# Gathering the 32-column matmuls of a LayerNorm backward stage into one place per pair of rows

## The chip, the cores and the metric

One core of one Trainium2 chip. The metric is the time of one execution in microseconds (us), as the device counts it; the lower the better. "Stage" below is the LayerNorm 2 backward stage, measured in a trace from the start of the last matmul of the gate and up projections in the main loop to the first matmul of the next transform. It is about 6% of the kernel.

## The reference, cut to what matters

The kernel computes a block with two LayerNorms, a spectral (FFT) filter and a gated bilinear feed-forward part, and all gradients of it. Only this much matters here:

```python
def _layernorm(x, axis=-1, eps=1e-05): ...
h = _layernorm(x) * (1 + ca) + sa
x = x + ga * _A_ref(h, A_w_r, A_w_i)       # rfft2 * W, irfft2
h = _layernorm(x) * (1 + cb) + sb          # LayerNorm 2
x = x + gb * _B_ref(h, ...)                # (h Wg) * (h Wu), times Wd
# reference = jax.vjp of this: the output and gradients by A_x, A_w_r, A_w_i,
# B_w_gate, B_w_up, B_w_down, c, w_mod; x is 2048 x 576
```

The backward stage of LayerNorm 2 takes the gradient by h, of 16 rows of tiles (128 x 576 each), and makes of it (1) column sums for the gradient of the modulation, (2) the gradient by x, multiplied and folded, whose (3) transform along the 16 rows of tiles starts the backward FFT.

Of the kernel before, what the change touches and what calls it, by code (L numbers as in the profile page):

```python
# [81 lines left out]
def build(ctx, tc, A_x, A_w_r, A_w_i, B_w_gate, B_w_up, B_w_down, c_in, w_mod, grad_out,  # L82
          out_0, out_1, out_2, out_3, out_4, out_5, out_6, out_7, out_8):
    nc = tc.nc
    pe, ve, ac, po, sp = nc.tensor, nc.vector, nc.scalar, nc.gpsimd, nc.sync
# [124 lines left out]
    with tc.manual_schedule(engines={PE}):  # L210
# [115 lines left out]
        def single():  # L326
            sbank[0] = (sbank[0] + 1) % 3
            return sbank[0]
# [112 lines left out]
        def stage_a(fj, b):  # L441
            for m in range(4):
                mm(bank[:, b, 128 * m:128 * m + 128], fj[:, FB[m]:FB[m] + 128], bdf, True, True)

        def stage_a_rem(fj, b, sub):
            mm(bank[0:32, b, 128 * sub:128 * sub + 128], fj[:, 256:288], bdf, True, True)
            mm(bank[32:64, b, 128 * sub:128 * sub + 128], fj[:, 544:576], bdf, True, True)

        def evac_a(eng, b, j):
            dst = At[:, 0:4, :, 8 * j:8 * j + 8]  # L450
            src = bank[:, b, :].rearrange("p (m c b) -> p m c b", m=4, c=16)
            if eng is ac:
                ac.copy(dst, src)
            else:
                ve.tensor_copy(dst, src)

        def evac_rem(eng, brem, j0, n):
            dst = At[0:64, 4, :, 8 * j0:8 * (j0 + n)].rearrange("p c (j b) -> p j c b", j=n)
            src = bank[0:64, brem, 0:128 * n].rearrange("p (j c b) -> p j c b", j=n, c=16)
            if eng is ac:  # L460
                ac.copy(dst, src)
            else:
                ve.tensor_copy(dst, src)
# [47 lines left out]
        def load_W(t, u):  # L511
            for ri, src in enumerate((A_w_r, A_w_i)):
                if u == 0:
                    rows = bass.AP(src.tensor, src.offset, [[16 * DF, 128], [8 * DF, 2], [1, DF]])
                    sp.dma_start(t[:, :, ri, 0:DF], rows)
                else:
                    sp.dma_start(t[:, 0, ri, 0:DF], src[u::16, :])
                    po.indirect_dma_start(out=t[:, 1, ri, 0:DF], out_offset=None, in_=src[:, :], in_offset=rev_rows, element_offset=(16 - u) * DF)
# [100 lines left out]
        for jg in range(4):  # L619
# [8 lines left out]
            for jj in range(4):  # L628
                b = single()
# [156 lines left out]
        def sbk():  # L786
            sbank[0] += 1
            return sring[sbank[0] % len(sring)]
# [148 lines left out]
        def acc_b(j):  # L937

            return acc[:, j, 0:288].bitcast(BF)
# [20 lines left out]
        def gh2_last(j):  # L960

            for h in range(2):
                b = sbk()
                gh2_mms(NP - 1, j, h, bank[:, b, 0:288])
                hs = slice(288 * h, 288 * h + 288)
                tt(acc_b(j)[:, hs], acc[:, j, hs], bank[:, b, 0:288], ADD)
# [57 lines left out]
        def quarter_sums(a, b, q, start, stop):  # L1024

            for h in range(2):
                r = slice(32 * (q + h), 32 * (q + h) + 32)
                mm(bank[r, b, 0:288], ones[:, 0:32], a[:, 288 * h:288 * h + 288], start, stop, skip_group_check=True)
# [14 lines left out]
        def load_n(j):  # L1043
            if j < 14:
                sp.dma_start(acc_h(j), n_d[:, j, :])

        def load_yl(i):
            yl[i] = yl_r.next()
            sp.dma_start(yl[i][:], y_d[:, 2 * i:2 * i + 2, :])
# [7 lines left out]
        def load_wdr(i0, i1):  # L1057
            sp.dma_start(wdr[:, i0:i1, :], B_w_down[128 * i0:128 * i1, :].rearrange("(j f) d -> f j d", f=128))
# [44 lines left out]
        st_a = {}  # L1103
# [4 lines left out]
        def front(i):  # L1108
            gn, t2, q, s = gn_r.next(), t2_r.next(), q_r.next(), s_r.next().rearrange("p (k v) -> p k v", k=2)
            n, opc = n_pair(i), two(mod[:, SCB, :])  # L1110
            tt(gn[:], b_pair(i), opc, MUL)
            tt(q[:], b_pair(i), n, MUL)
            tt(t2[:], q[:], opc, MUL)
            for k in range(2):
                j = 2 * i + k
                act(gn[:, k, :], gn[:, k, :], ACT.Copy, scale=rstd2[:, j:j + 1], accum_out=s[:, k, 0:1])
                act(t2[:, k, :], t2[:, k, :], ACT.Copy, scale=nrs2[:, j:j + 1], accum_out=s[:, k, 1:2])
            st_a[i] = (gn, t2, q, s)

        def back(i):  # L1120
            gn, t2, q, s = st_a[i]
            gx, n = gx_r.next(), n_pair(i)
            ts(s[:, :, 0], s[:, :, 0], -1.0 / D, None, MUL)
            for k in range(2):
                act(t2[:, k, :], n[:, k, :], ACT.Identity, bias=s[:, k, 0:1], scale=s[:, k, 1:2])
            tt(gn[:], gn[:], t2[:], ADD)
            tt(gx[:], gn[:], go[:, 2 * i:2 * i + 2, :], ADD)
            sp.dma_start(gx1_d[:, 2 * i:2 * i + 2, :], gx[:])
            tt(t2[:], gx[:], two(mod[:, SGA, :]), MUL)
            fold(gn, t2, 2)  # L1130
            tt(t2[:], gx[:], yl[i][:], MUL)

        def sums_1(j):
            quarter_sums(acc_b(j), 2, 0, j == 0, j == 15)
            quarter_sums(st_a[j // 2][2][:, j % 2, :], 2, 2, j == 0, j == 15)

        def sums_2(i):
            for k in range(2):
                quarter_sums(st_a[i][1][:, k, :], 5, 2 * k, i == 0, i == 7)

        def row_a(j):
            Fj = st_a[j // 2][0]
            b = sbk()
            stage_a(Fj[:, j % 2, :], b)
            evac_a(ac, b, j)
            if j % 2:
                b = sbk()
                for i in range(2):
                    stage_a_rem(Fj[:, i, :], b, i)
                evac_rem(ac, b, j - 1, 2)  # L1150

        def load_third(t, name, k):
            n = 1536
            sp.dma_start(t.rearrange("p a b c -> p (a b c)")[:, n * k:n * k + n], tabs[name][:, n * k:n * k + n])
# [6 lines left out]
        for j in range(19):  # L1161
            want = min(16, 3 + 5 * j // 4)
            while done < want:
                gh2_last(done)
                done += 1
                if done < want:
                    fill.run(1.0)
            while loaded < min(done, j + 6):
                load_n(loaded)
                loaded += 1  # L1170
            if j % 2 == 0 and j < 16:
                front(j // 2)
                back(j // 2)
                if 2 <= j < 14:
                    load_yl(j // 2 + 1)
            if fill.left() > 12.0 or j > 15:
                fill.run(1.0 if j < 16 else 2.0)
            if 1 <= j < 17:
                sums_1(j - 1)
            if fill.left() > 12.0 or j > 15:  # L1180
                fill.run(1.0)
            if 3 <= j:
                if j % 2 == 0:
                    sums_2(j // 2 - 2)
                row_a(j - 3)
            if j == 4:
                sp.dma_start(TB.rearrange("p a b -> p (a b)"), tabs["TB"][:, :])
            if 6 <= j < 9:
                load_third(TC, "TC", j - 6)
            if j == 12:  # L1190
                for i0 in range(9, 28, 5):
                    load_wdr(i0, min(28, i0 + 5))
                for k in range(3):
                    load_third(TI, "TI", k)
                sp.dma_start(TBI.rearrange("p a b -> p (a b)"), tabs["TBI"][:, :])
            if j == 15:
                for t in W_r.t:
                    po.memset(t[:, :, :, DF:FP], 0.0)
                for u in range(2):
                    Ws[u] = W_r.next()  # L1200
                    load_W(Ws[u], u)
            if j == 16:
                load_wdr(0, 6)
# [172 lines left out]
        for j in range(18):  # L1376
# [31 lines left out]
            while mdone < min(18, 6 * j // 5):  # L1408
                k, i = mdone // 3, mdone % 3
# [4 lines left out]
            if 5 <= j < 14:  # L1414
                i = j - 5
# [101 lines left out]
```

## The kernel before: the parts that the change and the argument touch

TensorE's order is the program's; the order of all other engines is chosen by a scheduler when the kernel is built. `fill` is a queue of matmul work left over from the main loop (weight gradients), drawn on here to keep TensorE busy. Its results need a PSUM bank from the same ring of six that the stage uses (`sbk`), and VectorE or ScalarE has to take them out (by a copy or a multiply) before the bank is free.

```python
def stage_a(fj, b):                       # 128-column matmuls
    for m in range(4):
        mm(bank[:, b, 128 * m:128 * m + 128], fj[:, FB[m]:FB[m] + 128], bdf, True, True)

def stage_a_rem(fj, b, sub):              # 32-column matmuls: the remainder of 576 = 4 x 128 + 2 x 32
    mm(bank[0:32, b, 128 * sub:128 * sub + 128], fj[:, 256:288], bdf, True, True)
    mm(bank[32:64, b, 128 * sub:128 * sub + 128], fj[:, 544:576], bdf, True, True)
# ...
def quarter_sums(a, b, q, start, stop):   # 32-column matmuls: column sums, kept in bank b
    for h in range(2):
        r = slice(32 * (q + h), 32 * (q + h) + 32)
        mm(bank[r, b, 0:288], ones[:, 0:32], a[:, 288 * h:288 * h + 288], start, stop, ...)
# ...
def front(i):                             # VectorE and ScalarE, a pair of rows at a time
    gn, t2, q, s = ...
    n, opc = n_pair(i), two(mod[:, SCB, :])       # n was stored by the main loop, and is loaded here
    tt(gn[:], b_pair(i), opc, MUL)                # L1111
    tt(q[:], b_pair(i), n, MUL)                   # L1112
    tt(t2[:], q[:], opc, MUL)                     # L1113
    for k in range(2):
        j = 2 * i + k
        act(gn[:, k, :], gn[:, k, :], ACT.Copy, scale=rstd2[:, j:j + 1], accum_out=s[:, k, 0:1])
        act(t2[:, k, :], t2[:, k, :], ACT.Copy, scale=nrs2[:, j:j + 1], accum_out=s[:, k, 1:2])
    st_a[i] = (gn, t2, q, s)

def back(i):
    # ... gn += n * s1 + s0 (ScalarE L1125, VectorE L1126); gx = gn + upstream gradient; stored
    tt(t2[:], gx[:], two(mod[:, SGA, :]), MUL)
    fold(gn, t2, 2)                               # L436, L437
    tt(t2[:], gx[:], yl[i][:], MUL)               # L1131

def sums_1(j):
    quarter_sums(acc_b(j), 2, 0, j == 0, j == 15)
    quarter_sums(st_a[j // 2][2][:, j % 2, :], 2, 2, j == 0, j == 15)

def sums_2(i):
    for k in range(2):
        quarter_sums(st_a[i][1][:, k, :], 5, 2 * k, i == 0, i == 7)

def row_a(j):
    Fj = st_a[j // 2][0]
    b = sbk()
    stage_a(Fj[:, j % 2, :], b)
    evac_a(ac, b, j)
    if j % 2:
        b = sbk()
        for i in range(2):
            stage_a_rem(Fj[:, i, :], b, i)
        evac_rem(ac, b, j - 1, 2)
# ...
for j in range(19):
    want = min(16, 3 + 5 * j // 4)
    while done < want:
        gh2_last(done)                            # a row of the gradient by h: 8 matmuls, 2 adds on VectorE
        # ... fill
    # ... loads of n for finished rows
    if j % 2 == 0 and j < 16:
        front(j // 2)
        back(j // 2)
    # ... fill
    if 1 <= j < 17:
        sums_1(j - 1)
    # ... fill
    if 3 <= j:
        if j % 2 == 0:
            sums_2(j // 2 - 2)
        row_a(j - 3)
    # ... loads of tables for the next stage
```

## Time and profile before

| | before |
|---|---|
| time, median of 3 runs | 1496.74 us (1494.34 to 1497.73) |
| span of the profiled run | 1493.0 us |
| stage in its trace | 87.3 us |

The page of the profiled run, cut to the span, TensorE's line and the chain that ended last (followed back from the last instruction; shares of the span):

```profile
span 1493.0 us, 28255 instructions
...
PE 1454.4 (97%) x11085; PEld 967.1 (65%) x11108; DVE 772.9 (52%) x1651; ACT 549.3 (37%) x1048; POOL 347.1 (23%) x510
...
## 4 chain that ended last, share of the span: by engine, by line
PE 82%; DVE 5%; DMA 5%; ACT 4%; issue 3%; POOL 1%; SPq 0%; DVEq 0%; ACTq 0%; POOLq 0%
```

(PE's count in before's trace is 23 short: some matmul records are missing there, while the weight loads, PEld, are 11108.) TensorE (PE) has work in flight nearly all the time, so the question is what its time consists of. The timeline of its matmuls in the stage shows the cost that the change aims at (columns: start in us, time in us, engine, source line, operation, out<-in, "rows*columns" of the array, output form, number of matmuls):

```profile
start us, us, engine line op out<-in xcount [idle before <-releaser]
...
1208.46 1.03 PE L885 MATMUL bank<-arena 128*128 128x256 bf16 x8
1209.42 0.31 PE L1028 MATMUL bank<-arena 128*32 128x288 bf16 x4
1209.66 1.05 PE L889 MATMUL bank<-arena 128*128 128x256 bf16 x8
1210.64 0.31 PE L1028 MATMUL bank<-arena 128*32 128x288 bf16 x4
1210.88 0.40 PE L443 MATMUL bank<-arena 128*128 128x128 bf16 x4
1211.21 0.23 PE L446 MATMUL bank<-arena 128*32 128x128 bf16 x1
...
1211.43 0.30 PE L944 MATMUL bank<-arena 128*128 128x288 bf16 x1
```

L1028 is the column sums (128*32: 32 columns), L443 `stage_a`, L446 and L447 its remainders, L885 and L889 are `fill`. Eight matmuls of L885 start at the usual pitch of 0.109 us, so the next could start at 1208.46 + 0.87 = 1209.33. The sums start at 1209.42, 0.09 later. Four sums run side by side in four column strips and would need 0.12 us (288 columns at the pitch of their 128-column neighbours), but 0.24 us pass until L889 may start. Together with 10 ns more behind the first matmul after it, one excursion into 32 columns costs about 0.22 us beyond its own data. The view of the sums' line shows the same on the row of weight loads (PEld): between like neighbours the next load starts 2 ns after a matmul's start, but the first load of a group of sums 0.20 us after it (durations are min/median/max in ns; the last line is idle time before, in us, and times):

```profile
L1028 PEld LDWEIGHTS <-arena x96: 92/93/93, 1195.2 to 1269.9; 128*32 128x32 bf16 x96
...
  issue: 5.2, 24
```

24 times 0.22 us. Two more views say what else goes on. First, busy time of each engine in windows of 5 us in the stage (columns: window, its length, then busy us and number of instructions of each engine, granted TensorE clock, share of the DMA engines, GB/s):

```profile
core 0: us, PE busy (x) PEld busy (x) DVE busy (x) ACT busy (x) POOL busy (x), PEclk, DMA share, GB/s
...
1228.00:1233.00 5.00, 5.00 (x53) 3.60 (x52) 1.88 (x5) 3.68 (x8) 0.00 (x0) 1.00 1.02 367
...
1238.00:1243.00 5.00, 2.28 (x23) 1.74 (x23) 5.00 (x13) 3.23 (x7) 0.00 (x0) 1.00 1.14 231
...
1253.00:1258.00 5.00, 5.00 (x61) 3.52 (x56) 4.93 (x9) 3.28 (x8) 4.40 (x6) 1.00 1.08 376
...
1263.00:1268.00 5.00, 5.00 (x52) 4.35 (x51) 1.00 (x3) 2.08 (x5) 0.79 (x1) 1.00 0.63 182
...
sum 80.00, PE 71.45 PEld 52.93 DVE 65.90 ACT 51.82 POOL 19.41; mean PE 4.47 PEld 3.31 DVE 4.12 ACT 3.24 POOL 1.21
```

VectorE (DVE) is busy 3.9 to 5.0 of every 5 us until 1263, with a hole at 1228 to 1233 (1.88), and idles mostly after that. Second, what TensorE waited for in the stage, and what VectorE waited for data from memory (columns: who, for whom: us in total, times, longest):

```profile
engine line waited for: us in total, times, longest us
PE bank L446 <- DVE arena L871: 2.7, 1, 2.7
PE bank L443 <- DVE arena L871: 1.9, 1, 1.9
PE bank L885 <- DVE arena L871: 1.8, 1, 1.8
PE bank L446 <- ACT arena L890: 1.3, 1, 1.3
PE bank L443 <- ACT arena L911: 0.6, 1, 0.6
PE bank L944 <- ACT arena L911: 0.2, 1, 0.2
```

```profile
DVE arena L1112 <- DMA arena<-n_d: 5.2, 4, 3.1
```

L870 and L871 are VectorE's multiplies that take `fill` results out of their banks, L890 and L911 are ScalarE's copies of such results. So TensorE stops for banks that the other two engines have not yet emptied, 8.5 us in all. L1112 is the multiply by n.

Below, the stage is split by the start times of its matmuls into three parts. *Array*: the columns streamed at the undisturbed pitch that the trace shows (122.5 ns per 288 columns, 109 per 256, 56 per 128; matmuls side by side counted once). *Switching*: the excess at places where the number of columns changes (32, 64 or 128), up to 0.13 us on the way in and 0.26 us for the group. *Waiting*: all the rest. For before this gives 70.0 + 8.0 + 9.3 = 87.3 us.

### The profile page before, as it was taken

To read this page: it belongs to the slowest core of one execution; us is meant where nothing else is said; L and a number is where in the kernel's file an instruction comes from. 1 tells how busy PE (TensorE), PEld (TensorE's weight loads), DVE (VectorE), ACT (ScalarE), POOL (GpSimd) and SP (SyncE) were. 2 spreads that over 40 slices of the span, in tenths; PEclk is the share of its full clock that TensorE was granted. 3 is DMA by queue.
4 is the path that set the end of the run, shared out by engine and by line. 5 is a ranking of instruction groups with operands and counts; after the bars stand their busy time and mean duration, and the time that the engine had idled before them with its cause. 6 is when DMAs were issued, how large, how long until landed. Compare 5 with 4: busy or idle time off the path is not lost.

```text
span 1493.0 us, 28255 instructions
## 1 busy us (share of the span) xinstructions
PE 1454.4 (97%) x11085; PEld 967.1 (65%) x11108; DVE 772.9 (52%) x1651; ACT 549.3 (37%) x1048; POOL 347.1 (23%) x510
## 2 busy tenths in 40 slices
PE   8999999999999999999999999999999998999998
PEld 5444444677677677677677677677677666677666
DVE  6533596533533533533533533533533688677665
ACT  6756675212212212212212212212212266334566
POOL 1344322213113113113113113113112013242211
PEclk9999999999999999999999999999999999999999
DMA  9657996969567558569458467567467389677763
GB/s 346 178 148 160 231 236 167 211 138 176 127 123 186 120 120 183 121 123 186 120 121 185 120 122 184 121 123 183 116 124 164 78 226 300 238 206 196 236 230 101
DMA packets 417050, 252.79 MB, mean 169 GB/s; under 512 B 319730, under 2 KB 384692, under 8 KB 416660
## 3 DMA queue, kind: packets, MB, share of 16 engines
q1 hardware_dynamic: 388706, 166.53, 49.4%
q0 software_dynamic: 27440, 83.65, 18.4%
q8 instruction: 87, 1.43, 0.4%
q10 hardware_dynamic: 770, 0.80, 0.2%
q14 instruction: 47, 0.39, 0.1%
HBM read 98.52 MB, written 76.26 MB: 117 GB/s over the span
## 4 chain that ended last, share of the span: by engine, by line
PE 82%; DVE 5%; DMA 5%; ACT 4%; issue 3%; POOL 1%; SPq 0%; DVEq 0%; ACTq 0%; POOLq 0%
PE bank L807 9%; PE bank L838 8%; PE bank L809 8%; PE bank L885 8%; PE bank L889 8%; PE bank L1087 5%; PE bank L944 5%; PE bank L946 5%; PE bank L947 5%; PE bank L945 5%; PE bank L371 3%; PE bank L802 3%; PE bank L375 3%; PE bank L905 2%; DMA arena<-in_w_mod_dram 1%
## 5 line engine op out<-in xcount | busy, mean ns | idle before, releaser
L958 DVE TENSOR_TENSOR arena<-arena,bank 128x576 f32<-128x576 f32 x256 | 193.0, 754 | 305.2 <-PE bank L947 305.2
L813 ACT CAST arena<-bank 128x512 bf16<-128x512 f32 x144 | 84.4, 586 | 384.7 <-PE bank L803 376.8
L947 PE MATMUL bank<-arena 128*128 128x288 bf16 x576 | 164.6, 286 | 0.0
L944 PE MATMUL bank<-arena 128*128 128x288 bf16 x576 | 164.0, 285 | 0.4 <-DVE arena L956 0.2
L946 PE MATMUL bank<-arena 128*128 128x288 bf16 x576 | 164.3, 285 | 0.0
L945 PE MATMUL bank<-arena 128*128 128x288 bf16 x576 | 164.1, 285 | 0.0
L1087 PE MATMUL bank<-arena 128*128 128x288 bf16 x1152 | 150.2, 288 | 3.4 <-ACT arena L1090 3.4
L885 PE MATMUL bank<-arena 128*128 128x256 bf16 x1152 | 149.5, 273 | 1.9 <-DVE arena L871 1.8
L889 PE MATMUL bank<-arena 128*128 128x256 bf16 x1152 | 149.3, 273 | 0.0
L807 PE MATMUL bank<-arena 128*128 128x512 bf16 x576 | 148.6, 380 | 0.0
L809 PE MATMUL bank<-arena 128*128 128x512 bf16 x576 | 147.8, 379 | 0.0
L1087 PEld LDWEIGHTS <-arena 128*128 128x128 bf16 x1152 | 112.1, 98 | 35.8 <-issue 7.3
L838 PE MATMUL bank<-arena 128*128 128x288 bf16 x1024 | 128.1, 286 | 0.0
L885 PEld LDWEIGHTS <-arena 128*128 128x128 bf16 x1152 | 110.8, 98 | 18.8 <-issue 5.2
L889 PEld LDWEIGHTS <-arena 128*128 128x128 bf16 x1152 | 112.3, 98 | 13.7
L838 PEld LDWEIGHTS <-arena 128*128 128x128 bf16 x1024 | 100.2, 98 | 28.2
L817 DVE TENSOR_TENSOR arena<-arena 128x512 bf16<-128x512 bf16 x144 | 61.1, 424 | 105.1 <-ACT arena L813 101.2
L735 POOL DMA_DIRECT2D arena<-ghh_d x36 | 20.0, 555 | 395.0 <-DVE arena L816 386.9
L890 ACT CAST arena<-bank 128x256 bf16<-128x256 f32 x144 | 52.6, 373 | 141.8 <-PE bank L889 141.8
L807 PEld LDWEIGHTS <-arena 128*128 128x128 bf16 x576 | 50.4, 98 | 78.3 <-issue 31.0
L809 PEld LDWEIGHTS <-arena 128*128 128x128 bf16 x576 | 56.4, 98 | 68.0
L814 ACT CAST arena<-bank 128x512 bf16<-128x512 f32 x144 | 84.8, 589 | 22.4 <-PE bank L809 22.4
(269 smaller groups left out, 2307.3 us busy)
## 6 DMA issues: line engine op xcount, KB each, us to landing
ghh_d<-arena POOLq DMA_DIRECT2D x72, 256.0 KB, 3.9
arena<-ghh_d POOLq DMA_DIRECT2D x36, 512.0 KB, 6.5
hh_d<-arena SPq DMA_DIRECT2D x36, 512.0 KB
arena<-hh_d SPq DMA_DIRECT2D x32, 576.0 KB
out_dram<-arena POOLq DMA_DIRECT2D x67, 144.0 KB, 4.5
out_dram<-arena POOLq DMA_DIRECT2D x36, 256.0 KB, 5.1
arena<-in_B_w_down_dram POOLq DMA_DIRECT2D x18, 288.0 KB, 4.3
arena<-in_B_w_gate_dram POOLq DMA_DIRECT2D x18, 256.0 KB, 3.5
```

The source lines that it names most:

```text
L807: mm(bank[:, bg, :], w[:, m, fs], h2T[:, js, m, :], odd == 0 and m == 0, odd == 1 and m == 3)
L809: mm(bank[:, bu, :], w[:, 4 + k, fs], h2T[:, js, m, :], odd == 0 and k == 0, odd == 1 and k == 3)
L814: ac.copy(u[:], bank[:, bu, :])
L838: mm(bank[:, b0 + h, 0:288], sf[:, 0, fb, j, :], go[:, j, 288 * h:288 * h + 288], j == 0, j == 15)
L885: mm(bank[:, st["b"], 0:256], h2p[:, j, 128 * m:128 * m + 128], sf[:, 1 + w, :, j, :], j == 0, False)
L889: mm(bank[:, st["b"], 0:256], h2p[:, j, 128 * m:128 * m + 128], sf[:, 1 + w, :, j, :], False, j == 15)
L944: mm(o, xT[:, 1, 0, cs], wT[p][:, 0, 0, hs], True, False)
L945: mm(o, xT[:, 2, 0, cs], wT[p][:, 0, 1, hs], False, False)
L946: mm(o, xT[:, 1, 1, cs], wT[p][:, 1, 0, hs], False, False)
L947: mm(o, xT[:, 2, 1, cs], wT[p][:, 1, 1, hs], False, True)
L958: tt(dst, dst, src, ADD)
L1087: mm(bank[:, yb, 0:288], hl[:, fb % 18, 128 * (j % 2):128 * (j % 2) + 128], wdr[:, fb, 288 * h:288 * h + 288], fb == 0, fb == 35)
```

## The change

The intent is to switch less often. The remainders of a pair of rows, its second sums, and the first sums of two rows are put one after the other; the count of matmuls is the same.

```diff
         def row_a(j):
-            Fj = st_a[j // 2][0]
             b = sbk()
-            stage_a(Fj[:, j % 2, :], b)
+            stage_a(st_a[j // 2][0][:, j % 2, :], b)
             evac_a(ac, b, j)
-            if j % 2:
-                b = sbk()
-                for i in range(2):
-                    stage_a_rem(Fj[:, i, :], b, i)
-                evac_rem(ac, b, j - 1, 2)
+
+        def rem_a(i):
+            b = sbk()
+            for k in range(2):
+                stage_a_rem(st_a[i][0][:, k, :], b, k)
+            evac_rem(ac, b, 2 * i, 2)
 # ...
             if fill.left() > 12.0 or j > 15:
                 fill.run(1.0 if j < 16 else 2.0)
-            if 1 <= j < 17:
-                sums_1(j - 1)
             if fill.left() > 12.0 or j > 15:
                 fill.run(1.0)
             if 3 <= j:
-                if j % 2 == 0:
-                    sums_2(j // 2 - 2)
                 row_a(j - 3)
+            if j % 2 == 0 and j >= 2:
+
+                if j >= 4:
+                    rem_a(j // 2 - 2)
+                    sums_2(j // 2 - 2)
+                if j < 18:
+                    sums_1(j - 2)
+                    sums_1(j - 1)
```

In the built programs the 128 matmuls of 32 columns stand in 32 separate places before and in 9 after. The scheduler answers with a new order on the other engines too, in this stage only: comparing the order of instructions in the two traces gives about 40 lines of difference on VectorE, 10 on ScalarE, 12 on GpSimd and 20 in the queue that issues loads.

More of the change, by code (lines that the diff above doesn't have):

```diff
@@ L1182, in build @@
             if 3 <= j:
-                if j % 2 == 0:
+                row_a(j - 3)
+            if j % 2 == 0 and j >= 2:
+                if j >= 4:
+                    rem_a(j // 2 - 2)
                     sums_2(j // 2 - 2)
-                row_a(j - 3)
+                if j < 18:
+                    sums_1(j - 2)
+                    sums_1(j - 1)
             if j == 4:
```

## The prediction

> What bounds the kernel. The page says the matmul row is busy 97% of 1493.0 us and 82% of the chain that ended last. The stage that changes is about 80 of those microseconds (1193 to 1273 us in the timeline). Cut into 5 us windows, VectorE is busy 3.9 to 5.0 of every 5 us from 1193 to 1258, except 1228 to 1233 (1.9), and idles only after 1263. Its waits there: 5.2 us for loads of n (4 times, longest 3.1), 1.4 for ScalarE; 5.8 for the last sums, at the end. TensorE meanwhile stands still about 9 us: 1.8 for a bank that VectorE has to empty (1202), 1.3 (1219.4), 2.7 (1238.5) and 1.9 (1244.7), 0.6 for a ScalarE copy (1258.6). So to about 1259 VectorE and the loads set the pace and TensorE is half a follower; from 1259 to 1273 the chain of waits is TensorE alone.
>
> What changes. No matmul is added or removed (the built programs have equal counts). The 32-column matmuls (96 sums, 32 remainders) stand in 32 separate places in the order before, in 9 after (mostly 4 remainders + 12 sums).
>
> Cost of a place. In the timeline four concurrent sums need 0.12 us (288 columns at the pitch of the neighbours), but between 128-column neighbours the last matmul before them takes 94 ns more to the next start than in an undisturbed row, the group itself 0.24 us instead of 0.12, and the first after them 10 ns more: 0.22 us extra. The weight row agrees: 24 loads of the sums stand 5.2 us on "issue". The Trainium skill, TensorEngine Tiling (Array Packing), Key Properties, says that a change of tiling mode drains TensorE; this trace agrees, with about 0.22 us per excursion. 23 fewer excursions: 23 x 0.22 = 5.1 us less TensorE time (estimate from those durations).
>
> What is on the critical path. Only the part that is not turned into longer waits for VectorE. TensorE's last stop is at 1258.6 to 1259.3, where it waits for a ScalarE copy that sits behind ScalarE work fed by VectorE. Behind it there are 5 excursions before and 2 after: 0.65 us, minus 0.12 for four sums that come later than before. Excursions ahead of it pay where TensorE feeds VectorE (banks to be evacuated, gradient rows). I expect about 40% of 5.1 us: 2 us. The scheduler also moves VectorE, the load queue and GpSimd in this stage (some twenty places on VectorE; the table and n loads in the queue). That may lengthen or shorten the waits for n by about 2 us either way. Nothing after the stage changes in order; the rest is TensorE-bound and passes the gain on.
>
> Prediction: 1494.8 us, 8 in 10 between 1491.0 and 1498.0. Faster by over 2%: 1%; within 2%: 98%; slower by over 2%: 1%.
>
> What would show each step. Right: weight loads of the sums standing on "issue" about 9 times for about 2 us instead of 24 and 5.2; excess per excursion still about 0.22 us; TensorE's waits for VectorE and ScalarE inside the stage grow from 9 to about 12 us; VectorE's busy time is unchanged (65.6 us); the stage is 1 to 3 us shorter. Wrong: TensorE's waits don't grow and the stage is 5 us shorter (TensorE did set the pace), or waits for n grow beyond 5.2 us and the gain is gone.
>
> What would make it wrong: the new VectorE order putting a multiply by n ahead of its load; late sums holding the q buffers (two of them), so that VectorE waits for TensorE; the sums at the very end delaying their copies into the next stage; run-to-run spread, 3.4 us among three runs before.

## The result, and the profile after

| | before | after |
|---|---|---|
| time, median | 1495.74 us (1494.34 to 1497.73, 4 runs) | 1492.55 us (1492.22 to 1496.84, 4 runs) |
| ratio to before | | 0.9984, 95% interval 0.9962 to 1.0007 |
| span of the profiled run | 1493.0 us | 1490.5 us |
| stage | 87.3 us | 85.3 us |
| of it array / switching / waiting | 70.0 / 8.0 / 9.3 us | 70.0 / 3.2 / 12.1 us |

A ratio here and below is the mean time of one kernel's fast runs over that of before's fast runs of the same rounds, so it is not quite the ratio of the medians quoted.

```profile
span 1490.5 us, 28274 instructions
...
PE 1451.7 (97%) x11108; PEld 967.7 (65%) x11108; DVE 772.0 (52%) x1651; ACT 548.1 (37%) x1048; POOL 347.7 (23%) x510
```

(The followed chain of after breaks off early in its trace, so the shares of the two chains are not compared.) The timeline of one merged group, with the same columns as before:

```profile
1209.59 1.04 PE L889 MATMUL bank<-arena 128*128 128x256 bf16 x8
1210.47 0.39 PE L443 MATMUL bank<-arena 128*128 128x128 bf16 x4
1210.78 0.23 PE L446 MATMUL bank<-arena 128*32 128x128 bf16 x1
...
1210.80 0.30 PE L1028 MATMUL bank<-arena 128*32 128x288 bf16 x2
...
1210.90 0.54 PE L1028 MATMUL bank<-arena 128*32 128x288 bf16 x10
1211.37 0.30 PE L944 MATMUL bank<-arena 128*128 128x288 bf16 x1
```

Four remainders and twelve sums now lie together. From 1210.78 to 1211.37 they take 0.59 us, of which 0.11 + 0.37 is their own data; the entry (L443 holds 94 ns longer) and exit are paid once. The sums' own line no longer stands still, since the stop now falls to the first load of the group, a remainder's or one of its neighbours':

```profile
L1028 PEld LDWEIGHTS <-arena x96: 92/97/98, 1199.6 to 1268.8; 128*32 128x32 bf16 x96
...
  issue: 0.2, 1
```

What TensorE waited for in the stage, and VectorE's wait for n:

```profile
PE bank L446 <- ACT arena L890: 2.6, 1, 2.6
PE bank L885 <- DVE arena L871: 1.9, 1, 1.9
PE bank L443 <- ACT arena L911: 1.7, 1, 1.7
PE bank L443 <- DVE arena L871: 1.6, 1, 1.6
PE bank L446 <- DVE arena L871: 1.4, 1, 1.4
PE bank L443 <- ACT arena L890: 0.9, 2, 0.6
PE bank L885 <- ACT arena L890: 0.7, 1, 0.7
```

```profile
DVE arena L1112 <- DMA arena<-n_d: 3.1, 3, 1.7
```

The waits of TensorE went from 8.5 to 10.8 us by this view (9.3 to 12.1 by the start times). Windows of after: around its longest wait (1218), near the end of the stage, and the last but one:

```profile
1218.00:1223.00 5.00, 2.09 (x30) 1.47 (x29) 4.90 (x10) 5.00 (x13) 0.78 (x1) 1.00 0.95 211
...
1253.00:1258.00 5.00, 3.59 (x44) 2.81 (x43) 4.09 (x8) 4.58 (x12) 4.08 (x7) 1.00 1.08 382
...
1263.00:1268.00 5.00, 5.00 (x50) 4.51 (x49) 0.11 (x1) 1.60 (x4) 1.01 (x2) 1.00 0.86 266
...
sum 80.00, PE 69.00 PEld 55.07 DVE 65.88 ACT 52.31 POOL 20.67; mean PE 4.31 PEld 3.44 DVE 4.12 ACT 3.27 POOL 1.29
```

VectorE does the same work in both (sum 65.88 us against 65.90 over these 80 us) and fills the stage to about the same moment. Of the 4.9 us of switching that went away, 2.8 came back as waiting; 2.0 us of stage were won in this pair of traces. The rest of the 2.5 us in span comes from outside the stage, where nothing was changed: after is 0.4 us later at the stage's start and 0.9 us faster behind it, where before's trace has 3.4 us of halved TensorE clock at 1393.2 that after's has not. One pair is little: before's stage as it is was traced once, and the same stage of after took 85.3, 87.3, 85.4 and 87.6 us in the four traces that hold it unchanged (after, after_again, main_x32 and main_x128 below). So the 2.0 us are no larger than what the stage varies by from run to run.

### The profile page after: what moved, and what is told of

It is laid out like the page before. It is cut to its first block, busy times and chain, and to the rows that moved or that the text cites. A ratio compares the mean times of both kernels' runs of the same rounds, so it can differ in the third digit from the quotient of the medians.

```text
span 1490.5 us, 28274 instructions
## 1 busy us (share of the span) xinstructions
PE 1451.7 (97%) x11108; PEld 967.7 (65%) x11108; DVE 772.0 (52%) x1651; ACT 548.1 (37%) x1048; POOL 347.7 (23%) x510
## 5 line engine op out<-in xcount | busy, mean ns | idle before, releaser
L890 ACT CAST arena<-bank 128x256 bf16<-128x256 f32 x144 | 52.2, 372 | 135.1 <-PE bank L889 133.5
```

## The experiments

All ran on one core; right results unless stated. TensorE's list of matmuls in the stage is that of before or of after in all but `after_split` and `after_early` (which moves rows). This table shows every trace of the stage but those of `main_x32` and `main_x128`, which change the main loop alone (their stages, with after's order, took 85.4 and 87.6 us, with 3.4 and 6.8 us of half clock); "half clock" is the time within the stage in which the trace records a granted TensorE clock of 0.5, in stretches of 3.4 us or two of them end to end. Waiting includes what the half clock cost.

| run | stage | array | switching | waiting | half clock | ratio to before (95%) |
|---|---|---|---|---|---|---|
| before | 87.3 | 70.0 | 8.0 | 9.3 | 0 | |
| after | 85.3 | 70.0 | 3.2 | 12.1 | 0 | 0.9984 (0.9962 to 1.0007) |
| after_again | 87.3 | 70.0 | 3.2 | 14.1 | 6.8 | 0.9993 (0.9979 to 1.0008) |
| after_split | 89.8 | 70.2 | 8.7 | 10.9 | 6.8 | 0.9990 (0.9975 to 1.0004) |
| before_lite | 89.2 | 70.0 | 8.2 | 11.0 | 6.8 | 0.9998 (0.9985 to 1.0010) |
| after_lite | 81.8 | 70.0 | 3.2 | 8.7 | 3.4 | 0.9958 (0.9943 to 0.9973) |
| before_free | 79.4 | 70.0 | 7.8 | 1.6 | 0 | 0.9950 (0.9937 to 0.9963) |
| after_free | 78.3 | 70.0 | 3.1 | 5.3 | 0 | 0.9947 (0.9934 to 0.9961) |
| before_free2 | 80.0 | 70.0 | 7.9 | 2.2 | 0 | 0.9948 (0.9934 to 0.9963) |
| after_free2 | 80.7 | 70.0 | 3.1 | 7.7 | 3.4 | 0.9944 (0.9930 to 0.9959) |
| after_early | 86.1 | 70.0 | 3.2 | 12.9 | 10.2 | 0.9978 (0.9963 to 0.9993) |
| after_free3 | 73.7 | 70.0 | 3.1 | 0.6 | 0 | 0.9905 (0.9889 to 0.9922) |

### What one excursion costs: main_x32 and main_x128

In the main loop TensorE is fed without waits. One extra matmul in each of its 272 gradient rows, once with 32 columns and once, as the control, with 128:

```diff
                 gh2_mms(p, j, h, bank[:, b0 + h, 0:288])
+                if h == 0:
+                    mm(bank[0:32, b0, 288:416], ones[:, 0:32], ones[:], True, True)   # main_x32
+                    mm(bank[:, b0, 288:416], ones[:], ones[:], True, True)            # main_x128
```

(One of the two lines each.) Expected:

> The changed kernel with one extra matmul of 32 columns x 128 in each of the 272 gradient rows of the main loop (where TensorE is busy without waits), into columns of the bank that nothing uses; right results. It is alone between 128-column neighbours. With 0.22 us for the two changes of mode and 0.056 us for its own data it costs 272 x 0.27 = 74 us: about 1567 us. If the drain at a change of mode were not what costs (theory: the cost seen in the stage is that of waiting or of the small size itself), it costs as main_x128 does, about 15 us.

> Control for main_x32: the same extra matmul with 128 columns of weights, so that the tiling mode does not change; right results. 272 x 0.056 = 15 us by its data, up to 27 us if its weight load of about 0.1 us is not hidden: 1508 to 1520 us.

One run each: 1562.70 us (4 us below what I expected) and 1509.04 us (in the expected range), both correct (state unknown, being single runs). The main loop ends 70.1 us later than in after with the 32-column matmul and 12.7 us later with the 128-column one, so by the traces the same data cost (70.1 - 12.7) / 272 = 0.21 us more per matmul for the 32 columns alone. The timeline of main_x32, and then that of the control main_x128 at the same place:

```profile
500.95 0.29 PE L947 MATMUL bank<-arena 128*128 128x288 bf16 x1
501.17 0.23 PE L954 MATMUL bank<-arena 128*32 128x128 bf16 x1
501.33 0.30 PE L944 MATMUL bank<-arena 128*128 128x288 bf16 x1
```

```profile
500.53 0.22 PE L954 MATMUL bank<-arena 128*128 128x128 bf16 x1
500.59 0.29 PE L944 MATMUL bank<-arena 128*128 128x288 bf16 x1
```

A matmul with 128 columns of data holds the array for 0.056 us, as in the control; with 32 columns 0.16 us pass to the next start, and 0.22 from the last one before it where 0.12 is usual. This holds with nobody waiting for anything, so the 0.21 to 0.22 us belong to the change of tiling. (The matmul starts within 2 ns of its own weight load, and it is this load that starts late; what the array does in the meantime the trace doesn't show.) The Trainium skill, TensorEngine Tiling (Array Packing), Key Properties, says that a change of tiling mode drains TensorE; these runs agree and give it a price.

### Is the gain there at all, and does it go when only the switching comes back: after_again and after_split

`after_split` is after with a tiny 128-column matmul between the groups, 23 times, so that the mode changes as often as before. The order on VectorE, ScalarE and the load queue is instruction for instruction that of after.

```diff
+        def split():
+            mm(bank[:, 5, 320:336], ones[:], ones[:, 0:16], True, True)
 # ...
                     rem_a(j // 2 - 2)
+                    split()
                     sums_2(j // 2 - 2)
+                    if j < 18:
+                        split()
                 if j < 18:
                     sums_1(j - 2)
+                    split()
                     sums_1(j - 1)
```

> The changed kernel once more, with more rounds, beside the others of this call. Theory A (my prediction): the separate places of the 32-column matmuls cost TensorE about 0.22 us each, 23 fewer save about 5 us, and about 60% of that comes back as longer waits because VectorE paces the stage: ratio 0.9985, stage (last gate/up matmul to the first matmul of the next transform) about 85.3 us against 87.3. Theory N (noise): ratio 1.000 within 0.0007, and the stage's length varies by 2 us from run to run.

> The changed kernel with 23 tiny 128-column matmuls (16 columns of data, into unused columns of a bank) put between the groups of 32-column matmuls, so that the tiling mode changes as often as before, while VectorE's, ScalarE's and the load queue's order stay that of after, instruction for instruction. Theory A: switching in the stage goes from 3.2 back to about 8 us, waits fall from 12 to about 9.5, the stage is 2 us longer than after (87 us), ratio to before about 1.000. Theory R (the gain comes from the other engines' new order and not from the drains): the added switching is absorbed by waits, the stage stays at 85.3 us, ratio 0.9985. Theory P (TensorE paces the stage; the other engines' new order gave 3 us of the gain back): the stage is 5 us longer than after (90 us), ratio about 1.0018.

after_again: 1496.02 us against 1495.98 us of before (6 and 11 runs), ratio 0.9993; its stage took 87.3 us, 2 us more than in the first trace of the same program. after_split: 1495.33 us, ratio 0.9990. The two intervals overlap almost wholly, so by time alone neither the gain of after nor its loss by the split is established. Of my expectations, the ratios of theories A, R and N can't be told apart, and theory P's (1.0018) lies outside after_split's interval. Theory N was right in one thing: the stage's length does vary by 2 us. The traces say more. Both of these have 6.8 us of half clock in the stage (it cost about 2.8 us in one and 3.1 in the other, an estimate: half of the time in which TensorE had work during it), so they can be compared: switching 3.2 against 8.7 us, waiting 14.1 against 10.9, stage 87.3 against 89.8. Of 5.5 us of switching that came back (and 0.2 for the tiny matmuls), 3.2 were taken out of waits and 2.5 lengthened the stage (one trace each). That is the balance of before and after once more, with the other engines' order held fixed, and it speaks against the new order being the source of the gain. It remains one pair of traces.

The results of after_split were wrong in the gradients of c and w_mod: the small matmul, started with the "first" flag, fell into the bank (5) in which the second sums accumulate. The Trainium skill, PSUM — Partial Sum Buffer, The four PSUM rules, says that such a matmul clears the written-bits of the whole bank in the quadrants that it writes, so the next sum overwrites instead of adding. The wrong sums agree (relative error 0.97 and 0.96 there, 0.009 or less elsewhere). That the times don't depend on the values is taken for granted here and for the runs with wrong results below; no run tests it.

What made after's own stage 2 us longer is the clock. Windows of after_again (columns as before; the granted clock is the number after POOL):

```profile
1218.00:1223.00 5.00, 1.68 (x23) 1.00 (x21) 4.22 (x9) 5.00 (x12) 0.73 (x1) 0.78 0.89 198
1223.00:1228.00 5.00, 5.00 (x26) 3.42 (x25) 5.00 (x10) 3.09 (x8) 0.05 (x1) 0.54 1.09 278
```

TensorE waited 0.7 us from 1218.3 and 2.6 us from 1219.4 for ScalarE's copies, did about 1 us of work between 1217.4 and 1220.8, and from 1220.8 to 1227.6 its clock was halved: matmuls of 288 columns start every 0.24 us instead of 0.12. In the first trace of after the wait at the same place was as long (2.6 us, from 1218.8) and the clock stayed full. The Trainium skill, TensorE: Matmul & The Clock Gate, Part 1, says that the clock is halved after an idle window of 3413 ns, and that these windows run freely; the recorded stretches of 3.4 and 6.8 us agree, and so does the dependence on luck: where the wait falls in the window decides. "Idle" is too narrow, though. Cut all fourteen traces into windows of 3.413 us, on the grid that their clock changes lie on, and take of each window the share of time in which matmuls stream columns at the usual pitch. Of 5945 such windows at full clock (leaving out the first 30 and the last 5 us of a trace) all 26 with a share below 0.37 were followed by half clock, 4 more with 0.38 to 0.41 were too, and none above that. The long wait lies in one window in after_again (0.30) and is split over two in after (0.58 and 0.44).

How much of the spread between runs this explains is less clear. After's ten runs and before's of that job go with the mean clock that they recorded: after's have 1492.22 to 1493.26 us at 0.998 (four runs), 1494.17 at 0.996, 1495.99 to 1497.60 at 0.995 and below (five); before's runs of the same job as after_again 1493.55 to 1494.70 at 0.997 (three), 1495.09 and 1497.24 at 0.996 (two), 1495.88 to 1499.13 at 0.995 and below (six). At like clock after is about 1 us ahead, which is less than the spread. But over all jobs before ran from 1492.73 to 1497.07 us at one and the same 0.997, so the clock isn't the only source.

### Taking VectorE's work away: before_lite and after_lite

```diff
-            tt(t2[:], q[:], opc, MUL)
             # ...
-                act(t2[:, k, :], t2[:, k, :], ACT.Copy, scale=nrs2[:, j:j + 1], accum_out=s[:, k, 1:2])
+                act(t2[:, k, :], q[:, k, :], ACT.Copy, scale=nrs2[:, j:j + 1], accum_out=s[:, k, 1:2])
             # ...
             fold(gn, t2, 2)
-            tt(t2[:], gx[:], yl[i][:], MUL)
```

Wrong results, as in all runs named lite or free.

> Wrong results on purpose: before, with two VectorE multiplies of each pair of rows left out of the stage (t2 = q times the modulation row, and t2 = gx times y; about 16 x 0.67 = 10.7 us of VectorE). TensorE's list of matmuls is that of before. Theory A (VectorE paces the stage to about 65 us into it): the waits of TensorE shrink from 9.3 to 3 or less, the stage is about 5 to 7 us shorter (81 us), ratio about 0.996. Theory P (TensorE paces): stage within 1 us of before's 87.3, ratio 0.9995.

> Wrong results on purpose: the changed kernel with the same two VectorE multiplies left out. The question is the difference to before_lite, where VectorE has slack. Theory A: with VectorE out of the way the saved switching is no longer given back: stage 4 to 5 us shorter than before_lite's, ratio 0.0027 to 0.0033 below it. Theory R (gain from the new order of the other engines) or a gain that is bounded by something else than VectorE: the difference stays at 2 us (0.0015) or less.

before_lite: 1495.71 us, ratio 0.9998; my theory missed. With about 10.7 us less for VectorE (16 multiplies, 0.67 us from start to start; its busy time on the page fell by 8.2) nothing was won, so less work for VectorE is not enough by itself; that its amount plays no part is not shown, since this build also waited longer for n (below) and its stage had 6.8 us of half clock. after_lite: 1490.55 us, ratio 0.9958, and 5 us below before_lite in the median, more than I expected (ratio 0.0040 below it against 0.0027 to 0.0033, stage 7.4 us shorter against 4 to 5). So this pair doesn't show what I wanted of it. VectorE's waits for n, in before_lite and then in after_lite:

```profile
DVE arena L1112 <- DMA arena<-n_d: 7.1, 4, 4.0
```

```profile
DVE arena L1112 <- DMA arena<-n_d: 2.2, 2, 1.6
```

The loads are issued in another order in the two builds, and the waits for n alone differ by 4.9 us. before_lite also has one stretch of half clock more in its stage. How much of its 5 us is switching can't be told from these two runs.

### Taking the loads of n away as well: before_free and after_free

```diff
         def n_pair(i):
-            return acc[:, 2 * i:2 * i + 2, 288:576].bitcast(BF) if i < 7 else nrow
+            return go[:, 2 * i:2 * i + 2, :] if i < 7 else nrow
```

The loads still run; nobody in the stage waits for them.

> Wrong results on purpose: before_lite, and the stage's two readers of n take the resident rows of the upstream gradient in its place, so that nothing in the stage waits for the loads of n (they still run). before_lite was not faster than before, against my expectation: TensorE then waited for ScalarE's copies, and the waits for n had grown from 5.2 to 7.1 us. Theory L (the loads of n pace the middle of the stage, through VectorE and ScalarE's fixed order): waits of TensorE fall from 11 to 4 us or less, stage 81 to 83 us. Theory P (TensorE or something else paces): stage stays at 86 us or more.

> Wrong results on purpose: the same two edits on the changed kernel. With VectorE's work and the loads of n out of the way TensorE should pace the stage. Theory A: stage about 5 us shorter than before_free's (switching 3.2 against 8.2 us, waits alike), ratio 0.003 below it. Theory R (the gain is the other engines' order, not the drains): the difference is 2 us or less.

before_free: 1486.99 us, ratio 0.9950, stage 79.4 us, waiting 1.6, below even what theory L expected. So the late loads of n, together with VectorE's and ScalarE's work behind them, cause nearly all of TensorE's waits in before; without them TensorE paces that order, at 70.0 + 7.8 us. after_free: 1485.74 us, ratio 0.9947, stage 78.3. Here my theory failed: 4.7 us less switching made the stage 1 us shorter, and 3.7 us turned into waits (for ScalarE's copies L890 and L911, and VectorE's L871).

### Taking ScalarE's work away: before_free2 and after_free2

```diff
-                act(t2[:, k, :], q[:, k, :], ACT.Copy, scale=nrs2[:, j:j + 1], accum_out=s[:, k, 1:2])
             # ...
-                act(t2[:, k, :], n[:, k, :], ACT.Identity, bias=s[:, k, 0:1], scale=s[:, k, 1:2])
+                act(t2[:, k, :], n[:, k, :], ACT.Identity, bias=s[:, k, 0:1], scale=s[:, k, 0:1])
```

> Wrong results on purpose: before_free with one of ScalarE's two scaled sums per row left out as well (16 activations of about 0.86 us with the reading of the sum, 13.8 us of ScalarE's time in the stage). In before_free TensorE waited 1.6 us in the stage, so little is left to gain: stage 78.5 to 79.4 us, waits 1 to 1.6 us, switching about 8.

> Wrong results on purpose: the same on the changed kernel. In after_free the saved switching (4.7 us) came back as 3.7 us of waits, 2.9 of them for ScalarE's copies out of the banks (which stand behind its 0.8 us activations) and 1.3 for VectorE's. Theory A, in its amended form (the saving is real but goes to whichever of the other engines is next): waits fall from 5.3 to about 2.5, the stage is 3 to 4 us shorter than before_free2's, ratio 0.002 to 0.0027 below it. Theory R' (the merged groups themselves cause the waits, because 12 to 16 matmuls of one kind in a row fall at the wrong place): waits stay at 5 us and the difference at 1 us.

before_free2: 1489.85 us, ratio 0.9948, stage 80.0 us with 2.2 of waits: slightly above my range, and not faster than before_free. after_free2: 1488.86 us, ratio 0.9944; waiting 7.7 us, with 3.4 us of half clock in the stage. My expectation failed again, and the rival's (waits stay at 5 us) was nearer. Two readings stayed open: the merged order brings waits of its own, or the other engines are still too slow for a TensorE that needs only 73 us. In after_free VectorE was still busy 9.7 of 10 us from 1203 to 1213 and 9.1 from 1233 to 1243, which fits the second. (In before_free it was as busy there, 9.7 and 9.8, and TensorE, which had more of its own to do, waited only 1.6 us in all.)

### Taking nearly all of the row arithmetic away: after_free3

```diff
         def front(i):
-            gn, t2, q, s = gn_r.next(), t2_r.next(), q_r.next(), s_r.next().rearrange(...)
-            ...                                   # 2 multiplies and 2 activations
-            st_a[i] = (gn, t2, q, s)
+            gn, t2 = gn_r.next(), t2_r.next()
+            tt(gn[:], b_pair(i), two(mod[:, SCB, :]), MUL)
+            st_a[i] = (gn, t2, go[:, 2 * i:2 * i + 2, :], None)
         def back(i):
-            ...                                   # scale, 2 activations, add
+            gn, t2, q, s = st_a[i]
+            gx = gx_r.next()
             tt(gx[:], gn[:], go[:, 2 * i:2 * i + 2, :], ADD)
             # ... store, multiply, fold as before
```

> Wrong results on purpose: the changed kernel with nearly all of the stage's row arithmetic left out (VectorE keeps the gradient rows, one multiply, one add, one multiply and the fold of each pair and the copies out of banks; ScalarE keeps only copies out of banks). TensorE's list of matmuls is that of after. The order before can't get under its 70.0 us of array time plus 8.0 us of switching, 78 us, whatever the others do; before_free was at 79.4 with 1.6 us of waits. Theory A amended (the saved switching is real TensorE time, and the waits for the other engines' copies take it): waits fall to 2.5 us or less and the stage is 74 to 76 us, below that floor; ratio 0.991 to 0.993. Theory R' (the merged groups bring 5 us of waits of their own, for instance by the moment at which a bank is asked for): waits stay at 5 us or more and the stage at 78 us or more.

1483.36 us against 1497.27, ratio 0.9905. Stage 73.7 us: array 70.0, switching 3.1, waiting 0.6. Ratio and stage lie just below theory A's ranges. The whole list of TensorE's waits in the stage:

```profile
PE bank L443 <- DVE arena L871: 0.4, 1, 0.4
```

Array and switching together come to 77.8 to 78.2 us in all four traces of before's order, however much it waited, and to 73.1 to 73.2 in the seven of after's in the table (without after_split). So by this account the order of before can't get below about 78 us whatever the others do; before with the same work taken away was not run. After's order, with its list of matmuls unchanged, ran in 73.7. So the 4.9 us are real TensorE time, the merged groups by themselves don't bring the waits, and what hides the saving in the real kernel is, by the lists of waits, the time until the other engines have emptied banks. That the groups ask for banks at worse moments when the other engines are loaded is not excluded. The Trainium skill, TensorEngine Tiling (Array Packing), PSUM Bottleneck, warns that tiling speeds up TensorE but not the evacuation of PSUM; the same happened here to time saved on switching.

### A try at a faster version: after_early

```diff
-            want = min(16, 3 + 5 * j // 4)
+            want = min(16, 4 + 3 * j // 2)
```

> A try at a faster version, right results: the changed kernel with the gradient rows finished in fewer iterations (4 + 3j/2 rows by iteration j in place of 3 + 5j/4), so that the loads of n, which need a row finished, are issued earlier. If the late loads of n hold the stage (before_lite and before_free say so) the waits for n go from 3.1 us to 1 or less and the stage gets 1 to 3 us shorter than after's 85.3: ratio 0.997 to 0.9985. If VectorE's own work holds it (65.9 of 80 us busy), or the earlier gradient rows push the first front further back, nothing is won: ratio 0.9985 to 1.000.

1493.64 us against 1496.82, ratio 0.9978 with an interval (0.9963 to 0.9993) that lies below 1. The waits for n fell only from 3.1 to 2.6 us, not to 1 as expected; in its trace TensorE waits 3.7 us at one place for a fold, and the stage, with 10.2 us of half clock in it, took 86.1 us and not less than after's 85.3. It has the lowest ratio of the correct kernels here, but its interval overlaps those of after's two measurements, so it can't be called faster than after, and the reason that I had given for it did not show.

## Why the prediction was right

- *Cost of a place, 0.22 us; 23 fewer, 5.1 us.* Right: switching fell by 4.9 us in the stage, and the excursion measured by itself in the main loop cost 0.21 us.
- *About 40% of it reaches the time, 2 us: 1494.8 us.* Right in size: the stage was 2.0 us shorter in the first pair of traces, and waits grew from 9.3 to 12.1 us (predicted: from 9 to about 12). The time, 1492.55 us, lies in the range. That says little: the range of 1491.0 to 1498.0 also holds before's own median, 1495.74, so no effect at all would have fitted too. The ratio's interval contains 1, so timing alone doesn't prove a gain; after_again gave 1496.02 us and 0.9993, and a stage of 87.3 us. That the first trace hit 2.0 us was partly luck with the clock.
- *VectorE's busy time unchanged.* Right, 65.9 us both times.
- *VectorE and the loads set the pace to about 1259.* Right only as a whole. Less work for VectorE alone gained nothing in before (before_lite: 10.7 us less of it); taking away the waits for the loads of n as well gained 8 us of stage (before_free). After still waits 5.3 us for VectorE and ScalarE without those loads (after_free), and hardly at all (0.6 us) once nearly all of their work is gone (after_free3).
- *The sums' weight loads stand still about 9 times for 2 us.* Wrong in form: once, 0.2 us. The groups begin with the remainders, so the stop shows on other lines.
- *Waits for n may move by 2 us either way.* They fell by 2.1 us, from 5.2 to 3.1, with the new order of the other engines. How much of the 2 us of stage is due to that stays open: after_split, with that order kept and the switching put back, gave 2.5 us of stage back, but in one pair of traces.
- *Run-to-run spread.* I named it and didn't know its source. Part of it goes with stretches of half clock, and some of these begin at the very waits that the change lengthens; before's runs at a clock of 0.997 still differ by 4.3 us, so the rest stays open.

## What to carry to other kernels

Price a change of tiling mode from the trace (the excess at the start times before, in and after the small group), and gather small matmuls where TensorE paces. Before counting the saving, look at what TensorE waits for in that stage: where it waits for banks, time taken off its own instructions can come back as longer waits, and long waits can cost the clock as well. To learn whether a saving is real, take the other engines' work away and see whether the stage falls below what the old order needs at least.

## What the Trainium skill lacked or had wrong

- TensorEngine Tiling (Array Packing), Key Properties, says that a change of mode drains TensorE but not what it costs: 0.21 us per excursion from 128 to 32 columns and back, measured in the main loop (57 us for 272), about 0.1 us on the way in and as much on the way out.
- TensorE: Matmul & The Clock Gate, Part 1, speaks of an idle window before the clock is halved. In after_again the clock was halved at 1220.8 us although TensorE had done about 1 us of matmuls in the 3.4 us before; its longest single wait was 2.6 us. A sparsely filled window is enough: over fourteen traces each of the 26 windows at full clock with less than 0.37 of matmul streaming was followed by half clock, and none with more than 0.41.
- The same part tells of such luck for the first matmuls of a kernel, and of half clock in the middle of kernels that wait for DMAs or cycle through PSUM banks. It doesn't say that the same luck adds to the spread between runs of a kernel that is busy otherwise: here six of the twelve stages in the table hold 3.4 to 10.2 us of half clock, with and without it for one and the same program, and after's ten runs range from 1492.2 us at a mean clock of 0.998 to 1497.6 at 0.992.
